# First weight slices of 128 columns and a first unit that contracts group 0 first, in a linear-attention and SwiGLU kernel

## The chip, the cores and the metric

The kernel runs on one core of one Trainium2 chip. The metric is the device time of one execution in microseconds (us), read as the median of several executions. Most executions of one kernel lie within about 0.3 % of each other, and the question here is about 0.1 to 0.4 %, so every comparison below uses runs of both kernels from the same rounds on the same chip.

Engine names in the profile: PE is TensorE's matmul, PEld its weight load, DVE is VectorE, ACT is ScalarE, POOL is GpSimd, SP is the engine that only issues transfers here. L283 means line 283 of the kernel; the changed kernel has two lines less, so L283 of before is L281 of after.

## The reference, cut to what matters

Eight batches of 8 heads, 576 positions of 64 channels. Attention is linear: softmax of q over the channels, softmax of k over the positions, then k-transposed times v, then q times that. The result x (4608 rows of 512) goes through a gated feed-forward network with d_ff = 1536.

```
q_s = softmax(q, axis=-1);  k_s = softmax(k, axis=2)
kv  = einsum('bhsd,bhse->bhde', k_s, v)
x   = einsum('bhsd,bhde->bhse', q_s, kv)      # -> (4608, 512)
g   = x @ w_gate;  val = x @ w_val
out = (g * sigmoid(g) * val) @ w_out
```

## The kernel before

The heads are worked in two groups of four ("group 0" and "group 1"); x of a group fills two of the four 128-row blocks of the contraction (`kk` 0 and 1 for group 0, 2 and 3 for group 1). Batch 0 is attended first. Its 576 tokens then go through twelve "units", each for 128 of the 1536 hidden columns: 16 matmuls with the gate and value weights, a SiLU on ScalarE, a multiplication on VectorE. That first run of twelve units is called the first chunk below. While it runs, the loads of batch 1 arrive, and the attention of batch 1 comes between the first chunk and the second.

Weights are float32 in HBM and bfloat16 in SBUF; the transfer converts them. They come in column slices, gate and value in turn, and then the output weights in four slices. The loads of batch 1 may not start before the second output-weight slice has landed (`after = w_dma[-3]`).

```python
for c0, n in ((0, 256), (256, 384), (640, 384), (1024, 512)):
    w_slice(wg, moe_w_gate, c0, n)
    w_slice(wv, moe_w_val, c0, n)
w_dma = [wo_slice(m0, 3) for m0 in (0, 3, 6, 9)]
# ... attention of batch 0 ...
after = w_dma[-3]
for what, src in (("q", q), ("v", v), ("k", k)):
    for G in range(NG):
        load(what, src, 1, G, after=after)       # only the first one carries the wait
        after = None
# ...
for m in range(MT):                              # the first chunk, twelve units
    m_unit(0, S, m, by_part=(m == 0))
exp_of("q", 1, 0); exp_of("q", 1, 1)             # batch 1, ScalarE; cut: sums on VectorE
i = norm_mul(1, 0)                               # q times 1/sum, VectorE
cast_v(1, 0); c = cast_v(1, 1)                   # v to bfloat16, GpSimd; c waits for i
o_out(0, o_mm(0), nc.scalar); o_out(1, o_mm(1), nc.scalar)
exp_of("k", 1, 0); turn_pe(1, 0, 0); turn_pe(1, 0, 1)      # transposes of q, TensorE
exp_of("k", 1, 1); norm_mul(1, 1); p = o_mm(2)   # cut: copies of the transposes
turn_pe(1, 1, 0); turn_pe(1, 1, 1)
kv_both(1)                                       # key-value products: need exp of k, v
# ... x of batch 1, then the second chunk
```

The softmax here doesn't subtract the row's maximum and nothing guards it: scores larger than these inputs give would overflow.

## Time and profile before

The median is 313.52 us over six runs (313.35 to 313.80). Here is what bounds it.

| What | before |
|---|---|
| Span of the profiled execution | 311.7 us |
| TensorE busy | 302.1 us, 97 % |
| First unit starts | 14.64 us |
| First output matmul (the first chunk is over) | 39.25 us |
| Second k piece of batch 1 lands | 46.28 us |
| Second chunk starts | 52.44 us |
| Last matmul ends | 307.50 us |

These lines are from the page of the kernel before: the span; each engine's busy time, share and instructions; TensorE's and the DMA engines' busy tenths in 40 slices of 7.8 us; and the packets, megabytes and share of the queue that carries the weights.

```profile
span 311.7 us, 5444 instructions
PE 302.1 (97%) x2182; PEld 150.1 (48%) x2182; DVE 160.3 (51%) x273; ACT 146.3 (47%) x214; POOL 28.9 (9%) x35
...
PE   6799999999999999999999999999999999999994
...
DMA  7999999999155906491729253605310202020034
...
q0 software_dynamic: 6640, 5.31, 11.0%
```

TensorE has gaps only in the first two slices, and the DMA engines are full from the second slice to the tenth (8 to 78 us). So TensorE is the limit from about 21 us on, and before that the weights are. Next is TensorE's own timeline: start, length, line, operation, output<-inputs, shapes and count, and in brackets the idle time before it with what ended it.

```profile
14.64 0.72 PE L283 MATMUL g_ps<-xt,wg 128*128 128x320 bf16 x4 [0.23 <-DMA wg<-in_moe_w_gate_dram]
15.98 0.72 PE L283 MATMUL u_ps<-xt,wv 128*128 128x320 bf16 x4 [0.62 <-DMA wv<-in_moe_w_val_dram]
...
17.40 1.14 PE L283 MATMUL g_ps<-xt,wg 128*128 128x320 bf16 x8
...
39.25 5.34 PE L308 MATMUL o_ps<-wo,hr 128*128 128x512 bf16 x24
44.68 0.68 PE L162 MATMUL tp<-ident,qs 128*128 128x128 bf16 x9
...
48.38 0.81 PE L187 MATMUL kv<-vb,ek 64*64 64x65 bf16 x72
...
52.44 0.54 PE L283 MATMUL g_ps<-xt,wg 128*128 128x448 bf16 x2
```

The two waits on weights stand in brackets. There is a third small one that carries no bracket: a half unit (8 matmuls) begins 0.98 us after the one before it, but the value half of the second unit begins at 20.62 after a gate half at 19.36, because its slice landed at 20.57. From the start of the first unit to that of the second it takes 17.40 - 14.64 = 2.76 us; an undisturbed unit takes 1.96 us. From 39 to 53 us TensorE waits for nothing.

How dearly a slice comes is seen from the issue view of the transfers, one narrow window for each: kilobytes (weights as written, in bfloat16; k in float32) and us from issue to landing. The first gate slice was issued at 8.67 us, the first value slice at 9.42 us, the second k piece at 35.97 us.

```profile
wg<-in_moe_w_gate_dram POOLq DMA_DIRECT2D x1, 256.0 KB, 5.9
...
wv<-in_moe_w_val_dram POOLq DMA_DIRECT2D x1, 256.0 KB, 6.5
...
k<-in_k_dram SPq DMA_DIRECT2D x1, 576.0 KB, 10.3
```

All landings together: 14.60 and 15.93 (256 columns), 18.63, 20.57, 22.54, 24.46 (384), 26.99 and 29.53 (512), 31.48 to 37.25 (output weights). Batch 1: loads issued from 33.38, q at 38.72 and 40.22, v at 41.71 and 43.20, k at 44.77 and 46.28.

### The profile page before, as it was taken

The numbers are of one execution on the slowest core, as the hardware profiler recorded it, in microseconds if no ns is written. First come the engines' busy times: TensorE is split into PE (matmuls) and PEld (weight loads), VectorE is DVE, ScalarE is ACT, GpSimd is POOL, SyncE is SP. The second block draws the span as 40 slices with busy tenths as digits, with TensorE's granted clock in tenths as the row PEclk, the third lists the DMA queues.
The fourth block names the chain that finished last, engine by engine and source line by source line (L and its number), as shares of the span: only waits on it lengthen the run. The fifth ranks groups of instructions, "written<-read, shape, count | busy, mean of one in ns | idle before, by whom it ended". The sixth has DMA issues, their size and how long they took to land.

```text
span 311.7 us, 5444 instructions
## 1 busy us (share of the span) xinstructions
PE 302.1 (97%) x2182; PEld 150.1 (48%) x2182; DVE 160.3 (51%) x273; ACT 146.3 (47%) x214; POOL 28.9 (9%) x35
## 2 busy tenths in 40 slices
PE   6799999999999999999999999999999999999994
PEld 2477745554444444454445444444444444444443
DVE  3834477945763567355836492639353324333321
ACT  5743378693764465547364637455143113312300
POOL 2930021321100110002000200000000000000000
PEclk9999999999999999999999999999999999999999
DMA  7999999999155906491729253605310202020034
GB/s 274 188 201 207 289 393 393 313 251 363 44 102 145 377 16 133 93 391 42 143 65 354 104 113 66 187 1 106 69 37 0 69 13 54 3 67 16 18 69 102
DMA packets 39305, 45.77 MB, mean 147 GB/s; under 512 B 16368, under 2 KB 23024, under 8 KB 39280
## 3 DMA queue, kind: packets, MB, share of 16 engines
q1 hardware_dynamic: 32480, 39.99, 43.3%
q0 software_dynamic: 6640, 5.31, 11.0%
q8 instruction: 17, 0.28, 0.4%
q10 hardware_dynamic: 160, 0.13, 0.2%
q14 instruction: 8, 0.07, 0.1%
HBM read 37.75 MB, written 9.44 MB: 151 GB/s over the span
## 4 chain that ended last, share of the span: by engine, by line
PE 84%; DMA 5%; DVE 4%; ACT 2%; issue 2%; POOL 1%; SPq 0%; DVEq 0%
PE o_ps L308 27%; PE g_ps L283 27%; PE u_ps L283 27%; DMA wv<-in_moe_w_val_dram 3%; DMA k<-in_k_dram 2%; DVE rs L133 1%; DVE hr L291 1%; PE xp L242 1%; DVE qs L147 1%; PE kv L187 1%; PE o_ps L328 1%; ACT L119 1%; ACT sg L290 0%; POOL wg L94 0%; POOL v L346 0%
## 5 line engine op out<-in xcount | busy, mean ns | idle before, releaser
L290 ACT ACTIVATE sg<-g_ps 128x512 bf16<-128x512 f32 (+2 forms) x120 | 64.8, 554 | 136.5 <-PE g_ps L283 134.3
L291 DVE TENSOR_TENSOR hr<-sg,u_ps 128x512 bf16<-128x512 bf16 (+2 forms) x120 | 74.3, 630 | 89.2 <-PE u_ps L283 83.3
L283 PE MATMUL u_ps<-xt,wv 128*128 128x512 bf16 (+2 forms) x480 | 111.3, 358 | 0.7 <-DMA wv<-in_moe_w_val_dram 0.6
L283 PE MATMUL g_ps<-xt,wg 128*128 128x512 bf16 (+2 forms) x480 | 111.4, 358 | 0.4 <-DMA wg<-in_moe_w_gate_dram 0.2
L308 PE MATMUL o_ps<-wo,hr 128*128 128x512 bf16 x420 | 93.8, 379 | 0.0
L283 PEld LDWEIGHTS <-wv 128*128 128x128 bf16 x480 | 46.8, 98 | 47.6 <-DMA wv<-in_moe_w_val_dram 1.4
L283 PEld LDWEIGHTS <-wg 128*128 128x128 bf16 x480 | 46.4, 98 | 45.7 <-DMA wg<-in_moe_w_gate_dram 0.5
L308 PEld LDWEIGHTS <-hr 128*128 128x128 bf16 x420 | 40.9, 98 | 48.7
L108 DVE COPY o_sb<-o_ps 128x512 f32<-128x512 f32 x32 | 21.8, 681 | 39.3 <-PE o_ps L308 39.3
L122 POOL CAST vb<-v 128x1152 bf16<-128x1152 f32 x14 | 16.9, 1205 | 138.1 <-DMA v<-in_v_dram 101.1
L133 DVE TENSOR_REDUCE rs<-eq 128x18 f32<-128x1152 bf16 (+2 forms) x18 | 21.7, 1214 | 12.9 <-ACT eq L119 12.9
L147 DVE TENSOR_TENSOR qs<-eq,rr 128x1152 bf16<-128x1152 bf16 (+2 forms) x18 | 21.7, 1216 | 0.1
L119 ACT ACTIVATE eq<-q 128x1152 bf16<-128x1152 f32 (+2 forms) x18 | 18.2, 1051 | 3.5 <-DMA q<-in_q_dram 3.4
L119 ACT ACTIVATE ek<-k 128x1152 bf16<-128x1152 f32 x16 | 18.0, 1160 | 0.2 <-DMA k<-in_k_dram 0.2
L290 ACT ACT_TABLE_LOAD x12 | 15.4, 1283 | 0.2
L119 ACT ACT_TABLE_LOAD x11 | 14.1, 1283 | 0.2
L256 ACT CAST xt<-xp 128x512 bf16<-128x512 f32 x14 | 7.9, 586 | 3.5 <-PE xp L242 3.5
L257 DVE CAST xt<-xp 128x512 bf16<-128x512 f32 x14 | 9.0, 683 | 0.9 <-PE xp L242 0.9
L373 PE MATMUL idle<-zero 128*128 128x512 bf16 x20 | 6.5, 480 | 2.7 <-DVE rs L133 1.5
L187 PEld LDWEIGHTS <-ek 64*64 64x64 bf16 x504 | 6.4, 107 | 1.3 <-ACT sg L290 0.4
L187 PE MATMUL kv<-vb,ek 64*64 64x65 bf16 x504 | 6.8, 194 | 0.0
L242 PE MATMUL xp<-qt,kn 64*64 64x512 bf16 (+1 forms) x112 | 6.7, 292 | 0.0
(43 smaller groups left out, 60.4 us busy)
## 6 DMA issues: line engine op xcount, KB each, us to landing
q<-in_q_dram SPq DMA_DIRECT2D x16, 576.0 KB, 5.2
k<-in_k_dram SPq DMA_DIRECT2D x16, 576.0 KB, 7.6
out_dram<-o_sb SPq DMA_DIRECT2D x70, 128.0 KB, 2.3
v<-in_v_dram SPq DMA_DIRECT2D x14, 576.0 KB, 8.4
wo<-in_moe_w_out_dram POOLq DMA_DIRECT2D x4, 384.0 KB, 16.5
wg<-in_moe_w_gate_dram POOLq DMA_DIRECT2D x2, 384.0 KB, 9.7
wv<-in_moe_w_val_dram POOLq DMA_DIRECT2D x2, 384.0 KB, 10.9
wg<-in_moe_w_gate_dram POOLq DMA_DIRECT2D x1, 512.0 KB, 13.9
```

The lines of the kernel that those rows point to most:

```text
L108: eng.tensor_copy(out=out, in_=in_)
L119: nc.scalar.activation(out=e[:, t0:t1], in_=src[:, t0:t1], func=AF.Exp)
L122: return nc.gpsimd.tensor_copy(out=vbs[G][:, :, :, 0:64], in_=raw["v", b, G].rearrange("p h (t d) -> p t h d", d=64),)
L133: i = nc.vector.reduce_sum(out=rs[:, 2 * t0:2 * t1], in_=eq2[:, 2 * t0:2 * t1, :], axis=mybir.AxisListType.X)
L147: last = eng.tensor_mul(qs[:, t0:t1, :].rearrange("p t (h d) -> p (t h) d", d=64), eq2[:, 2 * t0:2 * t1, :], s["rr"][:, 2 * t0:2 * t1].to_ ...
L187: nc.tensor.matmul(out=kv[g][HALF[h], c:c + 65], lhsT=ek[HALF[g], t, h, :], rhs=vbs[G][HALF[g], t, h, :], start=(t == 0), stop=(t == T - 1),)
L242: nc.tensor.matmul(out=o[h][HALF[g], c:c + 64 * (t1 - t0)], lhsT=kn[HALF[h], g, G, :], rhs=qt[G][HALF[h], t0:t1, 64 * g:64 * g + 64], star ...
L257: nc.vector.tensor_copy(out=xt[:, 2 * G + 1, c0:c0 + 512], in_=main[G][1])
L283: nc.tensor.matmul(out=gu[a][i][:, 0:w_], lhsT=(wg, wv)[a][:, kk, ms], rhs=xt[:, kk, c:c + w_], start=(kk == 0), stop=(kk == KT - 1),)
L290: nc.scalar.activation(out=sg[:, 0:w_], in_=g_ps[:, 0:w_], func=AF.Silu)
L291: nc.vector.tensor_mul(hr[:, m, r:r + w_], sg[:, 0:w_], u_ps[:, 0:w_])
L308: nc.tensor.matmul(out=o_ps, lhsT=hr[:, m, r0:r0 + 128], rhs=wo[:, m, :], start=(m == 0), stop=(m == MT - 1),)
```

## The change

The intent: the first unit should start sooner. Half as wide a first slice lands sooner, and a unit that contracts group 0 first needs group 1's x only half-way through. Its cost is more and smaller transfers. Cut to its core:

```diff
-    def m_unit(c0, n, m, by_part=False, by_group=False):
+    def m_unit(c0, n, m, by_group=False):
...
-        if by_part:
-            steps.sort(key=lambda a: (a[2], a[0], a[1]))
         if by_group:
-            steps.sort(key=lambda a: (a[1] // 2, a[0], a[1]))
+            steps.sort(key=lambda a: (a[1] // 2, a[0], a[2], a[1]))
...
-        for c0, n in ((0, 256), (256, 384), (640, 384), (1024, 512)):
+        for c0, n in ((0, 128), (128, 128), (256, 128), (384, 128), (512, 256), (768, 384), (1152, 384)):
...
+        kv_first(0)
         key_sum(1)
-        kv_first(0)
...
-        x_out(0, 0, 0, xp0[0], (nc.scalar, nc.scalar))
-        x_out(0, 0, 1, xp0[1], (nc.vector, None))
+        x_out(0, 0, 0, xp0[0])
+        x_out(0, 0, 1, xp0[1], (nc.scalar, None))
         scale_first(1, nc.vector)
+        x_out(0, 0, 1, xp0[1], (None, nc.vector))
         xp1 = x_mm(0, 1, 0), x_mm(0, 1, 1)
-        x_out(0, 1, 0, xp1[0], (nc.scalar, nc.vector))
-        x_out(0, 0, 1, xp0[1], (None, nc.vector))
-        x_out(0, 1, 1, xp1[1], (nc.scalar, nc.vector))
+        x_out(0, 1, 0, xp1[0])
+        x_out(0, 1, 1, xp1[1])
...
-            m_unit(0, S, m, by_part=(m == 0))
+            m_unit(0, S, m, by_group=(m == 0))
```

The eight transfers of gate and value weights become fourteen, which is six more issues on GpSimd. No arithmetic is added or taken away.

## The prediction

> **What bounds the kernel now.** TensorE is busy 97% of the 311.7 us span (page, part 1); its real gaps lie in the first 21 us (timeline). From 8 to 55 us the DMA engines are busy in nearly every slice (DMA row of the page), at about 400 GB/s read. So the start is bound by arriving weights, then TensorE runs dense.
>
> Landings (DMA issue view): second v piece 13.2 us, gate slice 0 14.57, value slice 0 15.92, gate slice 1 18.65, value slice 1 20.57. A 256-column slice thus costs about 1.36 us of DMA, 384 columns 1.94, 512 columns 2.5. The expert units start at 14.64 and stall for slice 0 (0.23 and 0.62 us) and for value slice 1 (0.41); each takes 1.96 us of TensorE, and the chunk ends at 39.14.
>
> **The change.** (1) Per matrix, four 128-column slices come first; in cost they replace the 512-column one. (2) The first unit contracts group 0 first, whose x copies move ahead of those of group 1. (3) Key-value products of group 0 go before the second key sum; the x products still follow the transposes, so I expect nothing from it.
>
> **Cost of a 128-column slice (estimate).** The three costs lie on a line, 0.58 us per 128 columns plus 0.2, which gives 0.76 us. The Trainium skill, "DMA: Bandwidth & Descriptors", section "Why small descriptors are slow", says about 3 extra cycles per packet; with 512 B read per row that agrees. Its "Specifications" warn of read-modify-write below 512 B, and the new rows write 256 B. This trace has no such write: the main risk.
>
> **Start of the chunk (estimate).** Gate slice 0 lands at 14.0, value slice 0 at 14.8, then one slice every 0.76 us, faster than the 0.98 us of TensorE that each feeds. The first matmul starts at about 14.6, held by the products of group 1 ahead of it, and the three stalls vanish. The chunk ends near 38.15: 1.0 us earlier.
>
> **Where it is given back.** All weights cost 2 x (4 x 0.76 - 2.5) = 1.1 us more DMA time. Loads of batch 1 start when the second output-weight slice has landed (33.3), so they land 1.1 us later. Before, k of batch 1 lands at 44.7 and 46.2, its exponentials start at 45.11 and 46.75, the products that need them at 48.38. That slack is about 0.9 us, against 1.0 (TensorE earlier) plus 1.1 (loads later). The exponential of q (landed 38.7, now 39.8) also starts only 0.6 us earlier. So over half of the gain becomes a new TensorE wait at 43 to 49 us. Later TensorE is dense and keeps what is left: 0.3 to 0.6 us.
>
> **Prediction.** 313.1 us, range 312.2 to 314.6 (the upper end if 256 B writes cost as much as 512 B ones; then weights fall behind TensorE, too). Faster by over 2%: 0.01; within 2%: 0.975; slower by over 2%: 0.015.
>
> **What would show it.** Right: small slices landing about 0.76 us apart (DMA issue view); the first unit's matmuls from about 14.6 without a DMA wait, chunk end near 38.2 (timeline); new TensorE idle of 0.3 to 1 us between 43 and 50 us (waits); batch 1 loads issued near 34.4 instead of 33.4. Wrong: slices over 1 us apart, weight waits in units 1 to 6, loads issued after 35.5.
>
> **What would make it wrong.** Small rows costing more (slower than before) or nothing extra (up to 1 us faster); GpSimd, at 0.79 us per issue, becoming the limit for such small slices; a misread slack after 40 us.

## More of the kernel before

Last, the chain of waits between 40 and 50 us (start, length, what):

```profile
40.38 1.17 ACT eq L119
...
41.58 1.36 DVE rs L133
...
43.27 1.37 DVE qs L147
...
48.45 0.73 PE kv L187 x67
```

Batch 1 runs from q's exponential over VectorE to the transposes, and TensorE does the rest. No DMA is in it: k is in time.

## The result

The changed kernel takes 314.08 us (median of six runs, 313.68 to 314.33). The ratio to the kernel before is 1.0017, with a 95 % interval of 1.0004 to 1.0029. A ratio here is the mean time of one kernel's fast runs over that of the other's of the same rounds, so it is not quite the ratio of the medians. So the change costs about 0.5 us, inside the 2 % that count as the same, but on the slower side. These lines of its page answer to those of before:

```profile
span 312.1 us, 5426 instructions
PE 301.5 (97%) x2158; PEld 150.6 (48%) x2182; DVE 160.5 (51%) x273; ACT 146.2 (47%) x214; POOL 33.1 (11%) x41
...
q0 software_dynamic: 9808, 5.31, 12.4%
```

The queue of the weights moves the same 5.31 MB in half as many packets again, and the time that they took rises by 1.4 points (it counts packets that overlap, so it is no measure of the load; some of TensorE's matmul records are missing from this trace, 2158 of 2182; its weight loads are all there). TensorE's timeline of the changed kernel:

```profile
14.28 0.67 PE L281 MATMUL g_ps<-xt,wg 128*128 128x320 bf16 x4
14.78 0.65 PE L281 MATMUL u_ps<-xt,wv 128*128 128x320 bf16 x4
...
16.25 1.14 PE L281 MATMUL g_ps<-xt,wg 128*128 128x320 bf16 x8
...
37.81 5.34 PE L306 MATMUL o_ps<-wo,hr 128*128 128x512 bf16 x23
43.67 0.68 PE L162 MATMUL tp<-ident,qs 128*128 128x128 bf16 x9 [0.51 <-DVE qs L147]
...
47.58 0.48 PE L187 MATMUL kv<-vb,ek 64*64 64x65 bf16 x36
48.73 0.48 PE L187 MATMUL kv<-vb,ek 64*64 64x65 bf16 x36 [0.67 <-ACT ek L119]
...
52.47 0.54 PE L281 MATMUL g_ps<-xt,wg 128*128 128x448 bf16 x2
```

The start does what was intended: no wait for weights at all, and the first unit takes 1.97 us. But two new brackets stand between 43 and 49 us, where there were none. Following the same instruction in both timelines gives the lead of the changed kernel (its start subtracted from that of before):

| TensorE's step | before | after | lead |
|---|---|---|---|
| first unit | 14.64 | 14.28 | 0.36 |
| second unit | 17.40 | 16.25 | 1.15 |
| first output matmul | 39.25 | 37.81 | 1.44 |
| transposes of q, group 0 | 44.68 | 43.67 | 1.01 |
| transposes of q, group 1 | 47.79 | 46.97 | 0.82 |
| key-value products, group 0 | 48.38 | 47.58 | 0.80 |
| key-value products, group 1 | 48.69 | 48.73 | -0.04 |
| second chunk | 52.44 | 52.47 | -0.03 |
| last matmul ends | 307.50 | 307.52 | -0.02 |

The gain of 1.44 us is 0.36 from the earlier start, 0.79 from the first unit and 0.28 from the value slice that no longer comes late. (The earlier start is of this size in this execution only. Kernels with the start of before began at 14.64 to 14.80 in three profiles: before, E3, E8; those with narrow slices and the new order at 13.79 to 14.53.) All of it is gone by 48.73 us, and from there to the end TensorE is so dense that nothing is won or lost. The transfers say why. Small slices, from the issue view in two narrow windows (issued at 9.45, 10.18 and 10.91 us), and the instruction queue in the window from 14.5 to 17 us:

```profile
wv<-in_moe_w_val_dram POOLq DMA_DIRECT2D x1, 128.0 KB, 4.6
wg<-in_moe_w_gate_dram POOLq DMA_DIRECT2D x1, 128.0 KB, 4.8
...
wv<-in_moe_w_val_dram POOLq DMA_DIRECT2D x1, 128.0 KB, 6.1
...
q8 instruction: 1, 0.02, 2.4%
```

The slices land at 13.32, 14.09, 15.01, 17.06, 17.59, 18.30, 19.01, 19.75. Apart from the fourth, they are 0.53 to 0.92 us apart, and the last three 0.71 to 0.74. Nobody waits for the fourth, which comes 2.05 us after the third (its matmuls are due at 17.23). In that moment one packet of instructions, 16 KB, occupied a DMA engine for 2.4 % of 16 engines over 2.5 us, which is 0.96 us. The Trainium skill, "Runtime: NRT & Kernel Launch", section "Instruction fetch mechanics", says that instructions are fetched in blocks of 16 KiB by a DMA queue of their own and that the cost is mostly hidden. For the fetching engine it may be; here it may have been in the way of other transfers. That it delayed this slice is a reading of the two times, not something an experiment has isolated. But the two times go together in every kept trace: in each, the first such packet starts between 13.7 and 16.4 us, and one weight slice lands 0.3 to 1.7 us late 1.4 to 3.1 us after it. In before it is the second gate slice (packet at 15.56, landing at 18.63).

Batch 1 is loaded from 34.03 us (before 33.38), and q lands at 39.34 and 40.86, k at 45.85 and 47.35: 0.62 and 1.07 us later than before. The new waits in the view of waits between 36 and 53 us (engine, line, releaser: us in total, times, longest):

```profile
ACT ek L119 <- DMA k<-in_k_dram: 2.1, 1, 2.1
...
PE kv L187 <- ACT ek L119: 0.7, 1, 0.7
...
PE tp L162 <- DVE qs L147: 0.5, 1, 0.5
```

And the chain of waits now goes another way:

```profile
36.38 9.47 DMA k<-in_k_dram
...
45.87 1.16 ACT ek L119
...
47.61 1.07 ACT ek L119
```

Before, this stretch was bound by computing. Now it is bound by k: it lands, ScalarE takes the exponential of each piece, and TensorE waits for the second. An earlier start of the first chunk moves nothing on this path.

Two smaller terms can be read. First, q: its exponential begins 1.01 us earlier (39.37 instead of 40.38), held by q's landing for 0.43 us, and this takes the lead at the transposes from 1.44 to 1.01. Second, the second multiplication of q by its reciprocal sums took 1.71 us instead of 1.36, beside a GpSimd cast of v. E1 comes back to this.

This leaves a question. TensorE ends 0.02 us later, but the span is 0.4 us longer. The difference lies after the last matmul, in GpSimd's semaphore instructions that end the program (count, duration in ns, first and last start in us). One line for before, one for after:

```profile
L574 POOLq EVENT_SEMAPHORE  x4: 17/17/17, 310.8 to 311.6; - x4
```

```profile
L572 POOLq EVENT_SEMAPHORE  x4: 17/17/17, 310.8 to 312.0; - x4
```

They begin together and the last comes 0.4 us later. One step in between, after GpSimd has cleared its semaphores, takes 0.45 us instead of 0.08. The changed kernel has 69 GpSimd instructions, the one before 63 (the page shows 41 and 35, since it leaves out those that only wait, branch or signal).

### The profile page after: what moved, and what is told of

Read it like the earlier page. It is cut to its first block, busy times and chain, and to the rows that moved or that the text cites. A ratio compares the mean times of both kernels' runs of the same rounds, so it can differ in the third digit from the quotient of the medians.

```text
span 312.1 us, 5426 instructions
## 1 busy us (share of the span) xinstructions
PE 301.5 (97%) x2158; PEld 150.6 (48%) x2182; DVE 160.5 (51%) x273; ACT 146.2 (47%) x214; POOL 33.1 (11%) x41
## 3 DMA queue, kind: packets, MB, share of 16 engines
q0 software_dynamic: 9808, 5.31, 12.4%
## 4 chain that ended last, share of the span: by engine, by line
PE 80%; DMA 11%; ACT 2%; POOL 2%; issue 1%; SPq 1%; DVE 1%; DVEq 0%; ACTq 0%
PE o_ps L306 26%; PE g_ps L281 25%; PE u_ps L281 25%; DMA k<-in_k_dram 5%; DMA wo<-in_moe_w_out_dram 4%; DMA wv<-in_moe_w_val_dram 2%; PE kv L187 1%; PE xp L242 1%; ACT ek L119 1%; PE o_ps L326 1%; SPq L77 1%; POOL wv L94 1%; POOL wg L94 1%; DVE hr L289 0%; POOL v L344 0%
## 5 line engine op out<-in xcount | busy, mean ns | idle before, releaser
L306 PE MATMUL o_ps<-wo,hr 128*128 128x512 bf16 x404 | 92.6, 379 | 0.9 <-issue 0.2
L371 PE MATMUL idle<-zero 128*128 128x512 bf16 x20 | 7.8, 555 | 2.7 <-DVE rs L133 1.5
```

What stands on the lines that cost most here:

```text
L306: nc.tensor.matmul(out=o_ps, lhsT=hr[:, m, r0:r0 + 128], rhs=wo[:, m, :], start=(m == 0), stop=(m == MT - 1),)
```

## The experiments

My theory after the result (T): the extra DMA time of the small slices pushes k of batch 1 back by as much, since the DMA engines are never idle before it; k had only about 1.1 us of slack, and a start that is earlier uses up the same slack from the other side. Worked out from before: the second exponential of k started 0.47 us after k had landed at 46.28 (ScalarE was copying), and it ended, with 1.07 to 1.18 us, at about 47.9, while the products that need it started at 48.69. Without the copy in its way it would have been some 0.3 us earlier (an estimate), so k could have landed about 1.1 us later at no cost. Rivals: (R1) the reordering, not the slices, causes the loss; (R2) the late start of batch 1's loads, that is, the rule that releases them, is what matters, not the DMA time; (R3) the engines' own chain between 40 and 50 us (q's exponential, VectorE's multiplications, the transposes) gives the gain back whatever the loads do. A question apart is what the longer end of the program comes from.

One thing to know before the numbers: executions of one kernel differ by about 0.4 us (before: 313.35 to 313.80), and part of this can lie in the first 15 us: the first unit starts at 14.28 in the changed kernel and at 13.79 in E7, whose program is the same up to there. A profile shows one execution. So I compare positions within a profile, and times by their intervals. All twelve kernels gave the right result.

### E1: the slices alone

```diff
 (before)
-for c0, n in ((0, 256), (256, 384), (640, 384), (1024, 512)):
+for c0, n in ((0, 128), (128, 128), (256, 128), (384, 128), (512, 256), (768, 384), (1152, 384)):
```

> The kernel before with the 128-column slices alone; order of the first unit and of the x copies as before. Theory late k (the gain at the start is given back because k of batch 1 lands about 1.1 us later): the first expert chunk ends at 37.8 to 38.3 us instead of 39.14, k of batch 1 lands at 47.2 to 47.5 instead of 46.28, TensorE is level with the kernel before from 52 us on, and the time is that of the full change, 313.8 to 314.3. Rival (the engines' own chain between 40 and 50 us gives the gain back, whatever the loads do): the same times, so this run does not tell those two apart; it tells what the slices alone bring. If the slices were not the cause of the early start, the chunk would still end near 39.

Measured: 313.99 us (313.54 to 314.17), ratio 1.0008 (0.9993 to 1.0024). The first unit starts at 14.88 in this execution, and the first output matmul at 38.60. That is 0.65 us earlier than before and later than I had expected: the start itself came 0.24 us later in this execution, while from the first unit to the first output matmul it took 23.72 us instead of 24.61. k lands at 45.58 and 47.09, later than before by 0.8 and just outside what was expected (47.2 to 47.5). The second chunk starts at 52.62 (before 52.44): the lead is again gone. So the loss does not need the reordering, and R1 falls; but the way it went was another, that of R3: TensorE did not wait for k at all. These are VectorE's multiplication of q and GpSimd's cast of v in this run:

```profile
42.62 2.18 DVE L147 TENSOR_TENSOR qs<-eq,rr 128x1152 bf16<-128x1152 bf16 x1
```

```profile
42.46 1.14 POOL L122 CAST vb<-v 128x1152 bf16<-128x1152 f32 x1 [19.57 <-DMA v<-in_v_dram]
```

In before the same multiplication took 1.36 us, since the cast (41.77 to 42.91) was over by then. The Trainium skill, "SBUF — State Buffer", section "Who interferes with whom", says that a VectorE instruction with two SBUF inputs contends with a GpSimd instruction that reads SBUF, that whichever starts first holds the shared ports for its whole length, and that the other fully blocks. This trace agrees nearly: the cast had 0.98 us to go, and the multiplication took 0.82 us more. TensorE waited 0.92 us for it at the transposes. A program whose VectorE comes earlier, while v comes later, runs into this collision by its timing alone.

### E2: the order alone

```diff
 (after)
-for c0, n in ((0, 128), (128, 128), (256, 128), (384, 128), (512, 256), (768, 384), (1152, 384)):
+for c0, n in ((0, 256), (256, 384), (640, 384), (1024, 512)):
```

> The change without its narrow slices: first unit by group, x copies and key-value order as changed, slices as before. If the gain at the start comes from the slices: value slice 0 still lands near 15.9 and holds the first unit, the chunk ends at 39.0 to 39.3, loads as before, time within 0.2 us of the kernel before. If the order brings the early start: chunk end at or below 38.6.

Measured: 314.51 us (313.69 to 316.81), ratio 1.0042 (1.0007 to 1.0076). The first unit of the profiled execution:

```profile
17.67 0.84 PE L281 MATMUL u_ps<-xt,wv 128*128 128x320 bf16 x4 [2.41 <-DMA wv<-in_moe_w_val_dram]
```

The first value slice landed at 17.63 instead of 15.93, and TensorE stood for 2.41 us; afterwards the granted clock was 0.84 from 14 to 20 us and 0.88 from 20 to 26, and the chunk ended 3 us late. The other three executions had spans of 311.7, 312.0 and 313.1. So the order by itself brings no earlier start (14.60 against 14.64: the weights decide), and it is open to a late slice. How often this happens can't be said from four runs.

### E3: six more GpSimd instructions, and nothing else

```diff
 (before)
 w_dma = [wo_slice(m0, 3) for m0 in (0, 3, 6, 9)]
+pad = const.tile([128, 1], FP32, name="pad", tag="pad")
+for _ in range(6):
+    nc.gpsimd.memset(pad, 0.0)
```

> The kernel before with six tiny memsets more on GpSimd, right after its weight issues, where it is idle; nothing depends on them. Theory (the end barrier is 0.37 us longer in the changed kernel because GpSimd's program got six instructions longer): same TensorE timeline as before, the last GpSimd step of the end barrier takes 0.45 us instead of 0.08, time plus 0.3 to 0.4 us, 313.8 to 313.95. Rival (the longer end is chance of one run, or comes from the DMAs): time and end barrier as before, within 0.1 us.

Measured: 313.69 us (313.42 to 313.90), ratio 1.0003 (0.9990 to 1.0016). The end of its program, same view as above:

```profile
L577 POOLq EVENT_SEMAPHORE  x4: 17/17/17, 310.5 to 311.7; - x4
```

From the first to the last it is 1.2 us, as in the changed kernel, and not 0.8 as in before; the step in question took 0.44 us. So six more GpSimd instructions bring the longer end, memsets here as transfers there. The time, though, rose by only 0.1 us with an interval of 0.4 either way: the profile shows the step, the clock does not resolve what it costs. It has no part in the loss of the 1.44 us, which TensorE had lost long before.

The step isn't a matter of length. It took 0.43 to 0.45 us in all five profiles with 69 GpSimd instructions, 0.07 to 0.08 in the profiles with 63 and 64, and 0.08 again in the two with 79 (E9, E12). That would fit a boundary of fetched instructions that happens to fall there. The traces show a difference in the fetches that goes with it, but none that explains it. All five profiles with 69 have one 8 KB packet of instructions more than those with 63, and it starts 0.7 to 1.0 us after the step (311.77 to 312.99 us). E9 and E12 have theirs long before, at 175.02 and 173.38 us, and E8 (64) only 1.95 us after the step, at 314.81. No run isolates this.

### E4: release the loads of batch 1 earlier

```diff
 (after)
-after = w_dma[-3]
+after = w_dma[-4]
```

> The changed kernel with the loads of batch 1 released by the first output-weight slice instead of the second, so about 1.9 us earlier (near 32.1 us). Theory (the loads are late because the DMA engines have more work queued before them, so k lands when that work is done): k of batch 1 still lands at 47.0 to 47.5, time as the changed kernel, within 0.2 us. Rival (they are late because they are issued late): k lands near 45.5, TensorE is about 1 us ahead from 52 us on, time about 313.1.

Measured: 314.00 us (313.49 to 314.18), ratio 1.0011 (0.9997 to 1.0024). The piece of the chain of waits that holds k:

```profile
33.49 12.64 DMA k<-in_k_dram
```

And TensorE's timeline, from the first transposes of q on:

```profile
43.10 0.68 PE L162 MATMUL tp<-ident,qs 128*128 128x128 bf16 x9
...
47.37 0.48 PE L187 MATMUL kv<-vb,ek 64*64 64x65 bf16 x36 [0.50 <-ACT ek L119]
49.02 0.48 PE L187 MATMUL kv<-vb,ek 64*64 64x65 bf16 x36 [1.16 <-ACT ek L119]
```

The loads are issued from 31.54 us, 2.5 us earlier than in the changed kernel, and k still lands at 46.13 and 47.64 (before that edit 45.85 and 47.35); the last output-weight slice lands at 39.55 instead of 37.84. The engines were full already: bytes that go ahead of others only change places with them. R2 falls. What counts is the DMA work ahead of k, not the moment of its release. This run also speaks most clearly against R3 as the only cause: q comes in time, both of its multiplications take 1.36 us, and the transposes start 1.58 us before those of before, with no wait. The whole of this lead is then lost at the two waits for k's exponentials, 0.50 and 1.16 us, and the second chunk starts at 52.75 (before 52.44).

### E5: fewer and wider slices behind the first

```diff
 (after)
-for c0, n in ((0, 128), (128, 128), (256, 128), (384, 128), (512, 256), (768, 384), (1152, 384)):
+for c0, n in ((0, 128), (128, 128), (256, 256), (512, 512), (1024, 512)):
...
-w_dma = [wo_slice(m0, 3) for m0 in (0, 3, 6, 9)]
+w_dma = [wo_slice(m0, 6) for m0 in (0, 6)]
...
-after = w_dma[-3]
+after = w_dma[0]
```

> The changed kernel with less DMA work and fewer issues: per matrix only two 128-column slices, then 256, 512, 512, and the output weights in two halves (loads of batch 1 released by the first half, the same amount of weights as before). GpSimd has as many instructions as in the kernel before. Theory late k: the first chunk still ends at 37.6 to 38.3 us, k of batch 1 lands at 46.3 to 46.7 instead of 47.35, its last key-value products start at 47.8 to 48.1 instead of 48.73, TensorE is 0.6 to 1.0 us ahead of the kernel before from 52 us on, the end barrier is the short one, time 312.5 to 313.0. Rival (the engines' own chain gives the gain back whatever the loads do): level with the kernel before at 52 us, time 313.4 to 313.7.

Measured: 314.01 us (313.35 to 314.18), ratio 1.0011 (0.9999 to 1.0023): a miss. The DMA side went as expected, k at 45.14 and 46.64. But the weights were late (17.38 for the second value slice, 24.90 for the fourth), and TensorE waited for them, 0.16 us at 19.87 and longest here:

```profile
24.95 1.15 PE L281 MATMUL u_ps<-xt,wv 128*128 128x320 bf16 x8 [0.99 <-DMA wv<-in_moe_w_val_dram]
```

The first output matmul, at 39.66, is later than in before (39.25). I had costed the transfers and not the feed: a wide slice must land whole before its first unit starts, and a slice can come later than its neighbours' spacing says (the second value slice here by some 1.3 us, the first one in E2 by 1.7 us). The narrow slices of the change are insurance against this, and their price is the delay of k.

### E6 and E7: bring the exponential of k closer to its landing

The second piece of k is loaded and taken to its exponential in two parts, so that only the smaller part stands between the last landing and the products. E6 does this to E5, E7 to the changed kernel.

```diff
-load(what, src, 1, G, after=after)
+load(what, src, 1, G, BANKS if (what, G) == ("k", 1) else ((0, T),), after=after)
...
-exp_of("k", 1, 1)
+exp_of("k", 1, 1, BANKS)
```

> As the lean kernel, and the last k tile of batch 1 is loaded and exponentiated in two pieces (5 and 4 of 9 blocks), so that only about 0.55 us of ScalarE instead of 1.17 follow its last landing. Theory late k: 0.2 to 0.5 us more than the lean kernel, 312.2 to 312.7. If the k exponential is no longer what ends the wait there (DVE's chain for the transposes is), the same as the lean kernel within 0.15 us.

> The changed kernel with the last k tile of batch 1 in two pieces, its weights untouched. Theory late k: k still lands at about 47.35 us, but the last key-value products start near 48.1 instead of 48.73, TensorE is about 0.5 us ahead at 52 us, time 313.4 to 313.7 with the longer end barrier still there. Rival (the engines' own chain): no change, 314.0 to 314.2.

Measured: E6 313.55 us (313.37 to 314.45), ratio 1.0008 (0.9996 to 1.0019); E7 313.61 us (313.01 to 314.47), ratio 1.0007 (0.9991 to 1.0022). E6 missed: weights were late again (a wait of 0.43 us; first output matmul at 38.65), and its first multiplication of q took 1.81 us. In E7 the key-value products ended 1.65 us after the last piece of k had landed (48.21 against 46.56), 1.86 in the changed kernel (49.21 against 47.35). E7's profiled execution, from a start at 13.79, reached the second chunk at 51.46: from first unit to second chunk it took 37.67 us, before 37.80 and the changed kernel 38.19. So it mends the path in the profile by half a microsecond against the changed kernel, but the times of the four executions are too wide apart to show a gain over before.

### E8: more DMA work and nothing else

```diff
 (before)
+wo_ap = bass.AP(tensor=moe_w_out.tensor, offset=moe_w_out[0, 0].offset,
+                ap=[[d_model, 128], [128 * d_model, 3], [1, d_model]])
+more_w = const.tile([128, 3, d_model], BF16, name="more_w", tag="more_w")
+nc.gpsimd.dma_start(out=more_w, in_=wo_ap)
 w_dma = [wo_slice(m0, 3) for m0 in (0, 3, 6, 9)]
```

This loads one output-weight slice twice, the second time into a tile that nobody reads. The start and the units keep their form.

> The kernel before with one load more ahead of the output weights, of the size of an output-weight slice, into a tile that nothing reads: 1.9 us of DMA work and no other change. It delays the loads of batch 1 without any gain at the start. Theory late k: k lands near 48.2 instead of 46.28; of these 1.9 us about 1.1 are slack, so the last key-value products start at 49.5 to 49.7 instead of 48.79, TensorE is 0.7 to 0.9 us behind at 52 us, time 314.1 to 314.6. If k has more slack than that, time stays within 0.2 us of before.

Measured: 314.70 us (314.39 to 314.94), ratio 1.0039 (1.0026 to 1.0052), slightly above what was expected. The chain of waits:

```profile
36.84 9.90 DMA k<-in_k_dram
...
49.63 0.48 PE kv L187 x35
```

k lands at 46.74 and 48.25, 1.97 us later than before; a slice of output weights takes about 1.9 us. The second chunk starts at 53.36, 0.92 us later. So 1.97 us of delay cost 0.92 us of TensorE: about 1.05 us was slack, close to the 1.1 us that T had worked out. (TensorE waited 0.27 us at the transposes of q and 0.64 for k; the wait for k came last.) This is the cleanest test of T, since nothing else is touched: the route through k is shown, and the slack is measured.

### E9: all slices 128 wide

```diff
 (after)
-for c0, n in ((0, 128), (128, 128), (256, 128), (384, 128), (512, 256), (768, 384), (1152, 384)):
+for c0, n in tuple((128 * i, 128) for i in range(12)):
```

> The changed kernel with all twelve slices of each matrix 128 columns wide. Each costs about 0.73 us by the landings so far, so all weights take about 2 x (12 x 0.73 - 7.74) = 2.0 us more DMA time than before (the changed kernel: about 1). They still come faster than TensorE uses them (0.98 us per slice): first chunk ends at 37.5 to 38.5 us. Theory late k: k of batch 1 lands at 48.2 to 48.7, its last key-value products start at 49.5 to 50.1, TensorE is 0.7 to 1.3 us behind the kernel before at 52 us; with a long end barrier (79 GpSimd instructions, if the length matters at all beyond 69) 314.6 to 315.2. If narrow slices cost nothing at the end, it stays at 313.9 to 314.3, as the changed kernel.

Measured: 315.51 us (314.61 to 317.26), ratio 1.0070 (1.0045 to 1.0096); the profiled one is the fastest of the four. From the first unit (13.90) to the first output matmul (37.43) it takes 23.53 us, exactly as in the changed kernel, so more narrow slices feed TensorE no better. k lands at 46.63 and 48.14, later than in the changed kernel by 0.8. TensorE waits 1.8 us for q at the transposes and 0.6 us for k at the key-value products, and reaches the second chunk at 53.25, which is 0.8 us after before. More of the same change brings more loss, here by q as well as by k. The interval puts the loss at 1.4 to 3.0 us; the rest of it is not seen in the profile, which shows the fastest execution. I had expected its end of program to be long, with still more GpSimd instructions; it was short.

### E10 and E11: slices between the two, and the order of loads

```diff
 (after)
-for c0, n in ((0, 128), (128, 128), (256, 128), (384, 128), (512, 256), (768, 384), (1152, 384)):
+for c0, n in ((0, 128), (128, 128), (256, 256), (512, 384), (896, 640)):
... (output weights in two halves, and k in two parts, as in E6)
 E11 only:
-for what, src in (("q", q), ("v", v), ("k", k)):
-    for G in range(NG):
+for what, src, G in (("q", q, 0), ("v", v, 0), ("q", q, 1), ("v", v, 1), ("k", k, 0), ("k", k, 1)):
```

> The lean kernel with the two pieces of k, and its last three slices 256, 384 and 640 wide instead of 256, 512, 512, so that each lands before TensorE needs it. Expected: no weight wait over 0.2 us after the first unit, chunk end at 37.6 to 38.2, k lands at 46.4 to 46.8, last key-value products at 47.4 to 47.9, short end barrier, time 312.7 to 313.2. Rival: the DVE chain for the transposes (a q multiply slowed beside a v cast) holds TensorE instead; then level with the kernel before, 313.4 to 313.6.

> As e10, and batch 1 is loaded in the order q, v of group 0, q, v of group 1, k, k, so that both v casts run beside DVE's reductions and not beside its multiplies. Expected: both multiplies of q at 1.36 us, the v casts at 1.15 us, last key-value products at 47.0 to 47.6, TensorE 1.0 to 1.5 us ahead at 52 us, short end barrier, time 312.2 to 312.8. If q of group 1, now 1.5 us later, becomes the wait instead, no better than e10.

Measured: E10 313.55 us (313.20 to 313.85), ratio 1.0002 (0.9990 to 1.0014); E11 313.44 us (312.97 to 314.02), ratio 0.9996 (0.9983 to 1.0009). Both missed. In E10 the collision of E1, and with it R3, returned: a multiplication of 2.18 us and a wait of 0.91 us at the transposes. In E11, where v of group 0 comes before q of group 1 so that its cast is over in time, both multiplications took 1.36 us; the order of loads does cure the collision. But in both the weights were late (first output matmul 38.70 and 39.08), so there was little to gain.

### E12: narrow slices for longer, the order of loads, and k in two parts

```diff
 (after)
-for c0, n in ((0, 128), (128, 128), (256, 128), (384, 128), (512, 256), (768, 384), (1152, 384)):
+for c0, n in ((0, 128), (128, 128), (256, 128), (384, 256), (640, 384), (1024, 512)):
...
+pad = const.tile([128, 1], FP32, name="pad", tag="pad")
+for _ in range(12):
+    nc.gpsimd.memset(pad, 0.0)
... (order of loads as in E11, k in two parts as in E7)
```

The twelve idle instructions bring GpSimd to 79, with which E9 had the short end of program.

> What the runs so far suggest together: the changed kernel with slices of 128, 128, 128, 256, 384 and 512 columns (every one due at least 1.4 us before TensorE needs it, for one DMA engine is about 1 us late in most runs), k of group 1 in two pieces, loads in the order q, v, q, v, k, k, and twelve idle memsets that bring GpSimd's program to 79 instructions, the length at which the all-128 kernel had the short end barrier. Expected: chunk end 37.5 to 38.0 us, k lands at 46.7 to 47.2, last key-value products end 1.64 us after it (as in e11), TensorE 0.3 to 0.7 us ahead at 52 us, end barrier 0.08 us, time 312.8 to 313.2, so faster than both kernels by 0.1 to 0.2%. If the barrier does not follow the program's length, it is the long one and the time 313.2 to 313.6.

Measured: 313.01 us (312.46 to 313.62, six runs) against 313.50 for before in the same rounds (eleven runs), ratio 0.9980 (0.9964 to 0.9996). By the 2 % rule it is the same; its interval lies below 1, and it is the only kernel here of which that is true (one of twelve such intervals, so the evidence is weak). In its timeline:

```profile
14.53 0.66 PE L281 MATMUL g_ps<-xt,wg 128*128 128x320 bf16 x4
...
38.06 5.34 PE L306 MATMUL o_ps<-wo,hr 128*128 128x512 bf16 x24
...
48.31 0.32 PE L187 MATMUL kv<-vb,ek 64*64 64x65 bf16 x16 [0.17 <-ACT ek L119]
...
51.88 0.54 PE L281 MATMUL g_ps<-xt,wg 128*128 128x448 bf16 x2
```

From the first unit to the second chunk it takes 37.35 us, against 37.80 in before and 38.19 in the changed kernel. There is no wait for weights, although the second gate slice came 1.4 us late (15.95), no slow multiplication, a wait for k of 0.17 us in place of 0.67, and a lead of 0.56 us at the second chunk; the step at the end took 0.08 us. Of the 0.56 us, 0.18 is left at the last matmul of this profile. The rest goes in small steps between 60 and 70 us. The waits between 53 and 80 us do not explain it: the only wait of TensorE for a transfer there, in the first line, is in before too, as long and at the same place, where the view gives it another label (second line).

```profile
PEld L242 <- DMA qt<-qs: 0.4, 1, 0.4
```

```profile
PEld L242 <- issue: 0.4, 1, 0.4
```

So where this lead is lost was not traced. E12 changes four things at once, and which of them earns how much was not separated.

## Why the prediction was right or wrong

**What was right.** The time was called the same within 2 %, and 314.08 lies in the range of 312.2 to 314.6. In its upper part that is luck: this was kept for 256 B writes that cost as much as 512 B ones, and they did not. The steps, one by one:

- *A 128-column slice costs 0.76 us.* Where nothing disturbed them they landed 0.71 to 0.77 us apart. The estimate came from a line through the costs of wider slices in the trace, and agreed with the Trainium skill, "DMA: Bandwidth & Descriptors", section "Why small descriptors are slow (HBM only)". That GpSimd's issues set the pace, which the prediction named as a risk, can be excluded: they came 0.73 us apart, but from issue to landing it took 4.6 us for the first slice and 5.9 us for the eighth, so transfers were queuing and the issues were ahead of them.
- *The read-modify-write below 512 B that its "Specifications" warn of is the main risk.* It did not show: rows of 256 B cost no more than the line gives.
- *The stalls vanish, the first unit starts at about 14.6.* They did; it started at 14.28.
- *Loads of batch 1 are issued near 34.4 and land 1.1 us later.* They were issued from 34.03, and k landed 1.07 us later. That the 1.1 was met is partly luck: the last weights landed only 0.59 us later than before and q 0.62 and 0.64. The rest came between the second q and the first v, which landed 1.96 us apart instead of 1.49, while a 16 KB packet of instructions occupied a DMA engine (40.61 to 41.65). What it would have been without this was not measured.
- *New TensorE idle of 0.3 to 1 us between 43 and 50 us.* There were 0.51 us for q, 0.67 us for k and 0.16 us behind them, 1.3 us in all: the kind was right, the size too small.

**What was mis-sized.** The chunk was to end at 38.15, 1.0 us earlier; the first output matmul came 1.44 us earlier. Of its terms, the start was to stay where it was and came 0.36 us earlier; the first unit was to lose a wait of 0.62 us and became 0.79 us shorter; the late value slice was put at 0.41 us, which was the wait of the weight load, while the matmuls behind it had lost only 0.28.

**The step that failed** is "Later TensorE is dense and keeps what is left: 0.3 to 0.6 us". That it is dense was right, and so it kept what was left; but nothing was left: the second chunk started at 52.47 against 52.44. The numbers for this were in the prediction. It gave k a slack of 0.9 us and a delay of 1.1 us. With a delay as large as the slack, the products can't come earlier than before, however early TensorE gets there, since k sets their time and not TensorE. I had split the lead into a lost half and a kept half, where the answer was the later of two times. The slack measured about 1.05 us (E8), the delay 1.07 us, and so the outcome is zero. That it is zero to within a few hundredths is partly luck: with k as late as q, by 0.64 us, some 0.4 us of lead could have been left (an estimate, 1.05 - 0.64). E8 shows this route with the delay alone, E4 shows that release is not what sets it and that k alone can take a lead of 1.6 us, and E9 shows that a larger delay (1.86 us) costs more. R3 is a second route beside it and not a rival that falls: in the changed kernel the lead went from 1.44 to 0.80 by q's later landing and the slowed multiplication, and only the last 0.84 at k; in E1 the slowed multiplication took it all.

**What was not foreseen** is the remaining 0.37 us at the end of the program, with six more GpSimd instructions. It makes up nearly the whole difference between the two profiled spans (0.40 us), and E3 reproduces it in a profile. Whether it is the whole 0.5 us of the timed difference stays open: E3's time rose by 0.1 us, within its interval. So the direction was wrong, too: 313.1 was a little below the time before, and the kernel came out a little above.

**What stays open.** Why the end of the program depends on how many instructions GpSimd has, and not on more or fewer; how late the late weight slice comes in each execution, and why; and which part of E12 earns its gain.

## What to carry to other kernels

An earlier start is worth what is left of it at the next place where data is awaited, so ask there for the later of two times, the engine's and the data's, and never subtract a share from the gain. Where transfers were dense up to that place, DMA work added ahead of it delayed its data by about as much (E8: a slice of 1.9 us, k 1.97 us later), and an earlier release did not help (E4: issued 2.5 us earlier, k 0.28 us later); measure the slack by adding one useless transfer. Where VectorE and GpSimd share a stretch, an order in which the cast is over before the two-input instruction starts can be worth trying: it kept the multiplication at 1.36 us here, against 2.18 us (E11 against E10).

## What the Trainium skill lacked or had wrong

- "DMA: Bandwidth & Descriptors", "Specifications": the read-modify-write below 512 B did not show in the cost of transfers that write 256 B rows to SBUF while they convert from float32. Slices of 128 columns landed 0.71 to 0.77 us apart, as a line through slices of 256, 384 and 512 columns (1.36, 1.94 and 2.5 us) gives. The page could say for which transfers it holds.
- "Runtime: NRT & Kernel Launch", "Instruction fetch mechanics": it has what a fetch costs the engine that fetches, and not that its 16 KB packet holds a DMA engine for 0.96 us. In this trace a weight slice landed 1.3 us later than its neighbours' spacing in that moment, and in each of the fourteen kept traces one slice lands 0.3 to 1.7 us late, 1.4 to 3.1 us after the start of such a packet (a reading of the times; no run isolates it).
- "SBUF — State Buffer", "Who interferes with whom": agrees in kind; the multiplication took 2.18 us instead of 1.36 when a cast had started 0.16 us before it. A full block for the rest of the cast would have made it 2.34 us.
- No page has the dependence of the program's end on GpSimd's instructions: a step of 0.43 to 0.45 us with 69 of them, 0.07 to 0.08 us with 63, 64 or 79.
